# A written issue order, a reciprocal root on VectorE and weights centred by matmuls, in a fused convolution and MLP kernel

## The chip, the cores and the metric

One core of a Trainium2 chip. The metric is the device time of one execution in microseconds (us); a kernel's figure is the median of its runs. All runs quoted here of one kernel lie within 0.15% of each other.

Names used below: PE is TensorE, PEld its weight loads, DVE VectorE, ACT ScalarE, POOL GpSimd, SP the sync engine that issues most transfers. "Span" is the profiled execution from first to last record; the run's time is some 2 us longer.

## The reference

```python
def _attn_ref(x, weight):                # x (8, 4224, 192), weight (8 heads, 7 taps)
    w = softmax(weight, axis=-1)         # shortened here
    x_pad = concatenate([zeros((B, 6, D)), x], axis=1)
    # ... a causal convolution of 7 taps along the sequence, one set of taps per 24 columns

def _moe_ref(x, g_ln, w_ch1, w_ch2):     # w_ch1 (192, 768), w_ch2 (768, 192), g_ln (192)
    mu = np.mean(x, axis=-1, keepdims=True)
    var = np.mean((x - mu) ** 2, axis=-1, keepdims=True)
    xn = (x - mu) / np.sqrt(var + 1e-06) * g_ln
    ch = np.maximum(xn @ w_ch1, 0.0) @ w_ch2
    return (x + ch).astype(np.float32)
```

The MLP weights arrive as 64-bit floats and are turned into 32-bit floats on the core. The mean need not be subtracted from x: both kernels put g and the subtraction into w1 ("centring": each column of g*w1 minus its mean), and multiply by 1/sqrt(var) after the down projection, since the ReLU commutes with a positive factor.

## The kernel before

The sequence is split into groups of 11 rows per partition, 24 groups. For each group DVE does the convolution (56 instructions), a 32x32 block transpose and the statistics; PE does `up` (w1 in four row quadrants of 32), ACT the ReLU, PE `down`, DVE the eviction with the factor and the residual.

```python
    def to_float32(dst, raw, n):            # 10 DVE instructions over n columns
        ...
    def prepare_w1():
        to_float32(w1f, raw1, NW1)          # NW1 = 1152
        ...                                 # share = g / D, a [128, 128] constant
        for r in range(2):
            ...
            nc.tensor.matmul(mean[r][:, 0:FH], share[:, 0, :], w1f[:, fs], start=True, stop=False)
            nc.tensor.matmul(
                mean[r][:, 0:FH], share[rows, 1, :], w1f[rows, F:NW1], start=False, stop=True
            )
        ...                                 # DVE: w1f = g * w1f - mean
        nc.sync.dma_start(out=w1c[0:P, :], in_=w1f[:, 0:F])       # w1c lies in DRAM
        ...
        for q in range(NQ):                 # and back, a copy for each quadrant
            (nc.sync, nc.scalar)[q % 2].dma_start(
                out=w1[C * q : C * q + C, :, :], in_=w1c.rearrange("(c d) f -> d c f", d=C)
            )

    def stats(g):
        ...
        nc.scalar.activation(r, v, AF.Sqrt, bias=eps)
        nc.vector.reciprocal(r, r)
        ...                                 # one Newton step on DVE

    def up(g):
        for f in range(NF):
            ph = [psum.tile([P, 512], F32, tag="ps", name=f"ph{g}_{f}_{q}") for q in range(NQ)]
            for c in range(NC):
                for q in range(NQ):
                    rows = slice(C * q, C * q + C)
                    nc.tensor.matmul(ph[q][:, 0:W], w1[rows, c, fs], t[rows, :, c, :], ...)
            ...                             # four ReLUs on ACT

    prepare_w1()
    conv(0); transpose(0); stats(0)
    to_float32(w2flat, raw2, NW2)
    for g in range(NG):                     # the framework's scheduler orders each engine
        load_x(g + 2); up(g)
        conv(g + 1); transpose(g + 1); stats(g + 1)
        down(g)
```

## Time and profile before

| | before |
|---|---|
| time, median of the first 3 runs | 1126.13 us |
| span of the profiled run | 1123.8 us |
| PE stream of 24 groups | 1036.9 us |
| first `up` matmul | 52.2 us |
| PE held in `up` of group 0 | 24.2 us |
| PE end to span end | 5.2 us |

PE is the bound from about 103 us on; all that a change can win without touching the matmuls of the groups is in the first 103 us and the last 5. The lines that carry this are in the prediction. A line of the timeline is read so: start, duration, engine, source line, operation, output<-inputs, form, count; then in brackets how long the engine was idle before it and who released it.

### The profile page before, as it was taken

To read this page: it belongs to the slowest core of one execution; us is meant where nothing else is said; L and a number is where in the kernel's file an instruction comes from. 1 tells how busy PE (TensorE), PEld (TensorE's weight loads), DVE (VectorE), ACT (ScalarE), POOL (GpSimd) and SP (SyncE) were. 2 spreads that over 40 slices of the span, in tenths; PEclk is the share of its full clock that TensorE was granted. 3 is DMA by queue.
4 is the path that set the end of the run, shared out by engine and by line. 5 is a ranking of instruction groups with operands and counts; after the bars stand their busy time and mean duration, and the time that the engine had idled before them with its cause. 6 is when DMAs were issued, how large, how long until landed. Compare 5 with 4: busy or idle time off the path is not lost.

```text
span 1123.8 us, 23187 instructions
## 1 busy us (share of the span) xinstructions
PE 1048.6 (93%) x10088; PEld 872.8 (78%) x10088; DVE 795.2 (71%) x2145; ACT 230.4 (21%) x603; POOL 9.1 (1%) x12
## 2 busy tenths in 40 slices
PE   1246999999999999999999999999999999999998
PEld 0126897887887887987987978978978878879877
DVE  5999778678587687696695796785886876875001
ACT  0012213113123123022122132131131131230220
POOL 0000000000000000000000000000000000000000
PEclk9987999999999999999999999999999999999999
DMA  7601211210211210211210211112102110000010
GB/s 263 165 1 61 100 60 54 85 61 41 99 60 41 99 60 40 99 61 41 99 61 40 85 62 54 60 54 86 60 40 99 61 40 40 1 40 40 1 40 39
DMA packets 10950, 72.85 MB, mean 65 GB/s; under 512 B 1640, under 2 KB 2536, under 8 KB 4704
## 3 DMA queue, kind: packets, MB, share of 16 engines
q1 hardware_dynamic: 8880, 67.63, 16.3%
q10 hardware_dynamic: 1968, 3.74, 1.2%
q8 instruction: 79, 1.29, 0.5%
q14 instruction: 23, 0.19, 0.1%
HBM read 44.82 MB, written 26.54 MB: 63 GB/s over the span
## 4 chain that ended last, share of the span: by engine, by line
PE 92%; DVE 6%; DMA 1%; ACTq 0%; ACT 0%; issue 0%; DVEq 0%
PE po L315 46%; PE ph L297 45%; DVE y L244 3%; DMA raw<-in_moe_w_ch_dram 1%; DVE st L261 1%; DVE yt L251 0%; DVE y L239 0%; PE mean L203 0%; PE mean L204 0%; DVE mant L154 0%; DVE scale L146 0%; DVE power L135 0%; DVE power L142 0%; DVE mant L150 0%; DVE rest L159 0%; DVE mant L158 0%
## 5 line engine op out<-in xcount | busy, mean ns | idle before, releaser
L297 PE MATMUL ph<-yt,w 32*128 32x352 f32 x6912 | 523.2, 458 | 46.4 <-ACT ht L302 24.2
L315 PEld LDWEIGHTS po<-w,ht 128*128 128x128 f32 x3168 | 513.5, 190 | 13.5 <-issue 11.8
L315 PE MATMUL po<-w,ht 128*128 128x192 f32 x3168 | 522.3, 327 | 0.0
L297 PEld LDWEIGHTS ph<-yt,w 32*128 32x128 f32 x6912 | 357.3, 186 | 205.1 <-ACT ht L302 24.8
L244 DVE SCALAR_TENSOR_TENSOR y<-xg,taps,y 128x264 f32<-128x264 f32 x1152 | 467.7, 485 | 0.0
L302 ACT ACTIVATE ht<-ph 128x352 f32<-128x352 f32 x576 | 220.4, 469 | 330.0 <-PE ph L297 330.0
L320 DVE SCALAR_TENSOR_TENSOR y<-po,r,y 128x192 f32<-128x192 f32 x264 | 95.0, 408 | 233.6 <-PE po L315 233.6
L272 ACT ACTIVATE r<-v,eps 128x11 f32<-128x11 f32 x24 | 7.3, 303 | 504.5 <-DVE y L320 454.5
L239 DVE TENSOR_SCALAR y<-xg,taps 128x264 f32<-128x264 f32 x192 | 54.8, 355 | 61.9 <-DMA out_dram<-y 61.9
L261 DVE BATCH_NORM_STATS2 st<-y 128x6 f32<-128x192 f32 x264 | 70.9, 344 | 0.8
L251 DVE STREAM_TRANSPOSE yt<-y 128x2112 f32<-128x2112 f32 x24 | 56.9, 2370 | 0.0
L203 PE MATMUL mean<-w1f,share 128*128 128x384 f32 x4 | 3.3, 928 | 23.6 <-DVE w1f L164 23.6
L203 PEld LDWEIGHTS mean<-w1f,share 128*128 128x128 f32 x4 | 1.0, 310 | 24.7 <-DVE w1f L164 23.6
L84 POOL MEMSET xg<- 1x1152 f32 x8 | 8.9, 1111 | 792.6 <-DVE y L244 792.3
L273 DVE RECIPROCAL r<-r 128x11 f32<-128x11 f32 x24 | 5.4, 225 | 8.1 <-ACT r L272 8.1
L135 DVE TENSOR_SCALAR power<-raw 128x1152 uint32<-128x1152 uint32 x2 | 1.5, 756 | 7.4 <-DMA raw<-in_moe_w_ch_dram 7.4
L277 DVE SCALAR_TENSOR_TENSOR d<-v,eps,d 128x11 f32<-128x11 f32 x24 | 5.5, 230 | 0.8
L272 ACT ACT_TABLE_LOAD x1 | 1.3, 1283 | 19.9 <-DVE y L244 19.9
L264 DVE TENSOR_TENSOR d<-st 128x11 f32<-128x11 f32 x24 | 4.2, 177 | 0.7
L280 DVE TENSOR_SCALAR d<-d 128x11 f32<-128x11 f32 x24 | 4.1, 172 | 0.8
L283 DVE TENSOR_TENSOR r<-r,d 128x11 f32<-128x11 f32 x24 | 4.1, 170 | 0.8
L276 DVE TENSOR_TENSOR d<-r 128x11 f32<-128x11 f32 x24 | 4.1, 169 | 0.8
(33 smaller groups left out, 40.9 us busy)
## 6 DMA issues: line engine op xcount, KB each, us to landing
xg<-in_x_dram SPq DMA_DIRECT2D x16, 1632.0 KB, 6.6
out_dram<-y SPq DMA_DIRECT2D x24, 1056.0 KB, 4.0
xg<-in_x_dram SPq DMA_DIRECT2D x8, 1056.0 KB, 5.3
xg<-in_x_dram SPq DMA_DIRECT2D x8, 504.0 KB, 6.2
raw<-in_moe_w_ch_dram ACTq DMA_DIRECT2D x1, 1152.0 KB, 12.5
w<-w1c SPq DMA_DIRECT2D x2, 576.0 KB, 10.0
w<-w1c ACTq DMA_DIRECT2D x2, 576.0 KB, 10.4
raw<-in_moe_w_ch_dram ACTq DMA_DIRECT2D x1, 768.0 KB, 7.5
```

Source lines behind the costliest of these rows:

```text
L84: nc.gpsimd.memset(t[0:1, 0:PAD, :], 0.0)
L239: nc.vector.tensor_scalar(out=y[g][:, :, cs], in0=t[:, 0:J, cs], scalar1=tap, scalar2=None, op0=ALU.mult,)
L244: nc.vector.scalar_tensor_tensor(out=y[g][:, :, cs], in0=t[:, k : k + J, cs], scalar=tap, in1=y[g][:, :, cs], op0=ALU.mult, op1=ALU.add,)
L251: nc.vector.transpose(yt[g].rearrange("p j c t -> p (j c t)"), y[g].rearrange("p j d -> p (j d)"))
L261: nc.vector.bn_stats(out=st[:, j, :], in_=y[g][:, j, :])
L272: nc.scalar.activation(r, v, AF.Sqrt, bias=eps)
L273: nc.vector.reciprocal(r, r)
L277: nc.vector.scalar_tensor_tensor(out=d, in0=v, scalar=eps, in1=d, op0=ALU.add, op1=ALU.mult)
L297: nc.tensor.matmul(ph[q][:, 0:W], w1[rows, c, fs], t[rows, :, c, :], start=(c == 0), stop=(c == NC - 1),)
L302: nc.scalar.activation(ht[g][:, f, :, q, :], ph[q][:, 0:W].rearrange("p (j t) -> p j t", t=C), AF.Relu)
L315: nc.tensor.matmul(dst, t[:, f, j, :, :].rearrange("p q t -> p (q t)"), w2[:, f, :], start=(f == 0), stop=(f == NF - 1),)
L320: nc.vector.scalar_tensor_tensor(out=y[g][:, j, :], in0=dst, scalar=rstd[g][:, j : j + 1], in1=y[g][:, j, :], op0=ALU.mult, op1=ALU.add,)
```

## The change

Its intent: start PE earlier, close the hole after group 0, shorten the end. Cut to its core:

```diff
+    sizes = [7, 8, rest // 2, rest - rest // 2]        # batch 0: 7, 8, 9, 9 rows
+    ctx.enter_context(tc.manual_schedule())            # the order of the source is kept
     ...                                                # w1 loaded in parts, x(0) before w2
-        ... 10 DVE instructions per conversion
+        ... 6 DVE and 2 ACT instructions (split_words, join_words)
-        mean matmuls, DVE corrections, to DRAM and back
+    m = setup.tile([P, NC, NQ, C], F32, name=f"centre{i}")   # mask: identity - 1/D, four times
+    nc.gpsimd.memset(m, -1.0 / D); nc.gpsimd.affine_select(m[p0:p1], ...)
+    nc.scalar.mul(flat, flat, gk)
+    def centre_w1():
+        for f in range(NF):
+            r, o = divmod(f * P, FH)
+            rows = slice(Q * r, Q * r + Q)
+            for c0, c1 in ((0, 4), (4, NC)):
+                pw = psum.tile([P, 512], F32, tag="ps", name=f"pw{f}_{c0}")
+                for c in range(c0, c1):
+                    dst = pw[:, (c - c0) * P : (c - c0 + 1) * P]
+                    nc.tensor.matmul(
+                        dst, centre[0][:, c, :], w1f[:, 1 + r, o : o + P], start=True, stop=False
+                    )
+                    nc.tensor.matmul(
+                        dst, centre[1][rows, c, :], w1f[rows, 0, o : o + P],
+                        start=False, stop=True,
+                    )
+                nc.scalar.copy(w1[:, c0:c1, f * P : f * P + P], ...)
     ...
-        nc.scalar.activation(r, v, AF.Sqrt, bias=eps)
-        nc.vector.reciprocal(r, r)
+        ... shift, subtract from 0x5F3759DF, three Newton steps, all on DVE
     ...
+        ends = (n,) if g + 1 < NG else (4, 8, 10, n)    # the last store in four pieces
     ...
-    prepare_w1(); conv(0); transpose(0); stats(0); to_float32(w2flat, raw2, NW2)
+    conv(0); centre_w1(); transpose(0)
+    parts = split_words(raw2, "2"); join_words(w2flat, raw2, *parts)
     for g in range(NG):
         ...
+        if g == 0: conv(1)
         up(g)
         if g + 1 < NG:
-            conv(g + 1); transpose(g + 1); stats(g + 1)
+            if g > 0: conv(g + 1)
+            transpose(g + 1)
+        stats(g)
         down(g)
```

w1 has 192 rows, 128 + 64, so each of its 36 outputs is the sum of a matmul over 128 rows and one over 64 rows.

More of the change, by code (lines that the diff above doesn't have):

```diff
@@ L9 @@
 U32 = mybir.dt.uint32
+I32 = mybir.dt.int32
 AF = mybir.ActivationFunctionType
@@ L53 @@
     NQ = P // C
-    W = J * C
-    assert D == P + Q and S % P == 0 and R % J == 0 and W <= 512 and NF % 2 == 0
-    groups = [(b, j0) for b in range(B) for j0 in range(0, R, J)]
+    FH = F // 2
+    assert D == P + Q and S % P == 0 and J * C <= 512 and NF % 2 == 0
+    groups = []
+    for b in range(B):
+        sizes = [J] * (R // J) + [R % J] * (R % J > 0)
+        if b == 0:
+            rest = R - 15
+            sizes = [7, 8, rest // 2, rest - rest // 2]
+        j0 = 0
+        for n in sizes:
+            groups.append((b, j0, n))
+            j0 += n
+        assert j0 == R and max(sizes) <= J
     NG = len(groups)
+    ctx.enter_context(tc.manual_schedule())
     xr = x.rearrange("b (p r) d -> b p (r d)", p=P)
@@ L64 @@
     setup = ctx.enter_context(tc.tile_pool(name="setup", bufs=1))
-    dram = ctx.enter_context(tc.tile_pool(name="dram", bufs=1, space=bass.MemoryType.DRAM))
     xpool = ctx.enter_context(tc.tile_pool(name="xin", bufs=3))
@@ L76, in load_x @@
     def load_x(g):
-        b, j0 = groups[g]
+        b, j0, n = groups[g]
         t = xpool.tile([P, J + PAD, D], F32, tag="xg", name=f"xg{g}")
@@ L81, in load_x @@
         if j0:
-            nc.sync.dma_start(out=flat, in_=xr[b, :, (j0 - PAD) * D : (j0 + J) * D])
+            nc.sync.dma_start(
+                out=flat[:, 0 : (n + PAD) * D], in_=xr[b, :, (j0 - PAD) * D : (j0 + n) * D]
+            )
             return
         nc.gpsimd.memset(t[0:1, 0:PAD, :], 0.0)
-        nc.sync.dma_start(out=flat[:, PAD * D :], in_=xr[b, :, 0 : J * D])
-        for p0, p1 in ((1, 16), (16, P)):
+        nc.sync.dma_start(out=flat[:, PAD * D : (PAD + n) * D], in_=xr[b, :, 0 : n * D])
+        for p0, p1 in ((16, P), (1, 16)):
             nc.sync.dma_start(
@@ L92, with load_w1 @@
     taps = consts.tile([P, H, K], F32, name="taps")
+    ga = consts.tile([P, 1], F32, name="ga")
+    gb = consts.tile([P, 1], F32, name="gb")
+    raw1 = setup.tile([P, 3, FH, 2], U32, name="raw1")
+    raw2 = setup.tile([P, NF * D, 2], U32, name="raw2")
+    w1_words = moe_w_ch1.bitcast(U32)
+    w2_words = moe_w_ch2.bitcast(U32)
+    g_col = moe_g_ln.rearrange("(d o) -> d o", o=1)
+    def load_w1(r):
+        nc.scalar.dma_start(
+            out=raw1[:, 1 + r, :, :].rearrange("p f w -> p (f w)"),
+            in_=w1_words[0:P, 2 * FH * r : 2 * FH * (r + 1)],
+        )
     nc.sync.dma_start(
@@ L95 @@
     )
-    FH = F // 2
-    NW1 = F + FH
-    NW2 = NF * D
-    raw1 = setup.tile([P, NW1, 2], U32, name="raw1")
-    raw2 = setup.tile([P, NW2, 2], U32, name="raw2")
-    ga = consts.tile([P, 1], F32, name="ga")
-    gb = consts.tile([P, 1], F32, name="gb")
-    w1_words = moe_w_ch1.bitcast(U32)
-    w2_words = moe_w_ch2.bitcast(U32)
-    g_col = moe_g_ln.rearrange("(d o) -> d o", o=1)
-    nc.scalar.dma_start(
-        out=raw1[:, 0:F, :].rearrange("p f w -> p (f w)"), in_=w1_words[0:P, :]
-    )
+    load_w1(0)
     for r in range(2):
         nc.scalar.dma_start(
-            out=raw1[Q * r : Q * r + Q, F:NW1, :].rearrange("p f w -> p (f w)"),
+            out=raw1[Q * r : Q * r + Q, 0, :, :].rearrange("p f w -> p (f w)"),
             in_=w1_words[P:D, 2 * FH * r : 2 * FH * (r + 1)],
         )
-    nc.scalar.dma_start(out=ga, in_=g_col[0:P, :])
+    load_w1(1)
+    load_x(0)
+    nc.gpsimd.dma_start(out=ga, in_=g_col[0:P, :])
     for r in range(2):
-        nc.scalar.dma_start(out=gb[Q * r : Q * r + Q, :], in_=g_col[P:D, :])
-    load_x(0)
-    load_x(1)
-    nc.scalar.dma_start(
+        nc.gpsimd.dma_start(out=gb[Q * r : Q * r + Q, :], in_=g_col[P:D, :])
+    nc.sync.dma_start(
         out=raw2.rearrange("p (c d) w -> p c (d w)", d=D),
@@ L125, with split_words @@
     )
-    def to_float32(dst, raw, n):
-        lo, hi = raw[:, :, 0], raw[:, :, 1]
-        power = setup.tile([P, n], U32, tag="power", name="power")
-        scale = setup.tile([P, n], U32, tag="scale", name="scale")
-        mant = setup.tile([P, n], U32, tag="mant", name="mant")
-        rest = setup.tile([P, n], U32, tag="rest", name="rest")
+    load_x(1)
+    low = consts.tile([P, 1], F32, name="low")
+    nc.vector.memset(low, -896.0 * (1 << 23))
+    def split_words(raw, name):
+        n = raw.shape[1]
+        hi = raw[:, :, 1]
+        mant = setup.tile([P, n], I32, name="mant" + name)
+        power = setup.tile([P, n], I32, name="power" + name)
+        high = setup.tile([P, n], F32, name="high" + name)
+        scale = setup.tile([P, n], I32, name="scale" + name)
+        nc.vector.tensor_single_scalar(mant.bitcast(U32), hi, 0xFFFFF, op=ALU.bitwise_and)
+        nc.scalar.activation(high, mant, AF.Relu, scale=2.0**-20, bias=1.0)
         nc.vector.tensor_scalar(
-            out=power, in0=hi, scalar1=20, scalar2=0x7FF,
+            out=power.bitcast(U32), in0=hi, scalar1=20, scalar2=0x7FF,
             op0=ALU.logical_shift_right, op1=ALU.bitwise_and,
@@ L139, in to_float32, with join_words @@
         nc.vector.tensor_scalar(
-            out=power, in0=power, scalar1=896.0, scalar2=0.0, op0=ALU.subtract, op1=ALU.max
+            out=power, in0=power, scalar1=896.0, scalar2=1151.0, op0=ALU.max, op1=ALU.min
         )
-        nc.vector.tensor_scalar(
-            out=power, in0=power, scalar1=255.0, scalar2=float(1 << 23),
-            op0=ALU.min, op1=ALU.mult,
+        nc.scalar.activation(scale, power, AF.Relu, scale=float(1 << 23), bias=low)
+        return high, scale
+    def join_words(dst, raw, high, scale):
+        lo, hi = raw[:, :, 0], raw[:, :, 1]
+        nc.vector.scalar_tensor_tensor(
+            out=high, in0=lo, scalar=2.0**-52, in1=high, op0=ALU.mult, op1=ALU.add
         )
         nc.vector.scalar_tensor_tensor(
-            out=scale, in0=hi, scalar=0x80000000, in1=power,
+            out=scale.bitcast(U32), in0=hi, scalar=0x80000000, in1=scale.bitcast(U32),
             op0=ALU.bitwise_and, op1=ALU.bitwise_or,
         )
-        nc.vector.tensor_scalar(
-            out=mant, in0=hi, scalar1=0xFFFFF, scalar2=3,
-            op0=ALU.bitwise_and, op1=ALU.logical_shift_left,
-        )
-        nc.vector.scalar_tensor_tensor(
-            out=mant, in0=lo, scalar=29, in1=mant,
-            op0=ALU.logical_shift_right, op1=ALU.bitwise_or,
-        )
-        nc.vector.tensor_single_scalar(mant, mant, 0x3F800000, op=ALU.bitwise_or)
-        nc.vector.tensor_single_scalar(rest, lo, 0x1FFFFFFF, op=ALU.bitwise_and)
-        nc.vector.scalar_tensor_tensor(
-            out=dst, in0=rest, scalar=2.0**-52, in1=mant.bitcast(F32),
-            op0=ALU.mult, op1=ALU.add,
-        )
-        nc.vector.tensor_tensor(dst, dst, scale.bitcast(F32), op=ALU.mult)
-    eps = consts.tile([P, 1], F32, name="eps")
-    nc.vector.memset(eps, 1e-6)
+        nc.vector.tensor_tensor(dst, high, scale.bitcast(F32), op=ALU.mult)
+    w1f = setup.tile([P, 3, FH], F32, name="w1f")
+    raw1a = raw1[:, 0:2].rearrange("p s f w -> p (s f) w")
+    raw1b = raw1[:, 2]
     wmax = consts.tile([P, H], F32, name="wmax")
@@ L176 @@
     nc.scalar.activation(taps, taps, AF.Exp)
+    parts_a = split_words(raw1a, "1a")
     nc.vector.tensor_reduce(wsum, taps, axis=AX.X, op=ALU.add)
@@ L182 @@
     )
-    w1f = setup.tile([P, NW1], F32, name="w1f")
+    join_words(w1f[:, 0:2].rearrange("p s f -> p (s f)"), raw1a, *parts_a)
+    parts_b = split_words(raw1b, "1b")
+    join_words(w1f[:, 2], raw1b, *parts_b)
     w1 = consts.tile([P, NC, F], F32, name="w1")
-    w2flat = consts.tile([P, NW2], F32, name="w2")
+    w2flat = consts.tile([P, NF * D], F32, name="w2")
     w2 = w2flat.rearrange("p (c d) -> p c d", d=D)
-    w1c = dram.tile([D, F], F32, name="w1c")
-    def prepare_w1():
-        to_float32(w1f, raw1, NW1)
-        share = setup.tile([P, 2, P], F32, name="share")
-        for i, g in enumerate((ga, gb)):
-            nc.vector.tensor_scalar(
-                out=share[:, i, :], in0=g.to_broadcast([P, P]),
-                scalar1=1.0 / D, scalar2=None, op0=ALU.mult,
-            )
-        mean = [psum.tile([P, 512], F32, tag="ps", name=f"mean{r}") for r in range(2)]
-        for r in range(2):
-            fs = slice(FH * r, FH * r + FH)
-            rows = slice(Q * r, Q * r + Q)
-            nc.tensor.matmul(mean[r][:, 0:FH], share[:, 0, :], w1f[:, fs], start=True, stop=False)
-            nc.tensor.matmul(
-                mean[r][:, 0:FH], share[rows, 1, :], w1f[rows, F:NW1], start=False, stop=True
-            )
-        for r in range(2):
-            fs = slice(FH * r, FH * r + FH)
-            rows = slice(Q * r, Q * r + Q)
-            nc.vector.scalar_tensor_tensor(
-                out=w1f[:, fs], in0=w1f[:, fs], scalar=ga, in1=mean[r][:, 0:FH],
-                op0=ALU.mult, op1=ALU.subtract,
-            )
-            nc.vector.scalar_tensor_tensor(
-                out=w1f[rows, F:NW1], in0=w1f[rows, F:NW1], scalar=gb[rows, :],
-                in1=mean[r][rows, 0:FH], op0=ALU.mult, op1=ALU.subtract,
-            )
-        nc.sync.dma_start(out=w1c[0:P, :], in_=w1f[:, 0:F])
-        for r in range(2):
-            nc.scalar.dma_start(
-                out=w1c[P:D, FH * r : FH * r + FH], in_=w1f[Q * r : Q * r + Q, F:NW1]
-            )
-        for q in range(NQ):
-            (nc.sync, nc.scalar)[q % 2].dma_start(
-                out=w1[C * q : C * q + C, :, :], in_=w1c.rearrange("(c d) f -> d c f", d=C)
-            )
@@ new lines @@
+    centre = []
+    for i, (gk, spans) in enumerate(((ga, ((0, P, 0),)), (gb, ((0, Q, P), (Q, P, P))))):
+        m = setup.tile([P, NC, NQ, C], F32, name=f"centre{i}")
+        nc.gpsimd.memset(m, -1.0 / D)
+        for p0, p1, base in spans:
+            nc.gpsimd.affine_select(
+                out=m[p0:p1], in_=m[p0:p1], pattern=[[-C, NC], [0, NQ], [-1, C]],
+                compare_op=ALU.not_equal, fill=1.0 - 1.0 / D, base=base, channel_multiplier=1,
+            )
+        flat = m.rearrange("p c q i -> p (c q i)")
+        nc.scalar.mul(flat, flat, gk)
+        centre.append(flat.rearrange("p (c o) -> p c o", c=NC))
@@ new lines, in centre_w1 @@
+    def centre_w1():
+        for f in range(NF):
+            r, o = divmod(f * P, FH)
+            rows = slice(Q * r, Q * r + Q)
+            for c0, c1 in ((0, 4), (4, NC)):
[4 more added lines that the diff above has]
+                        dst, centre[0][:, c, :], w1f[:, 1 + r, o : o + P], start=True, stop=False
+                    )
+                    nc.tensor.matmul(
+                        dst, centre[1][rows, c, :], w1f[rows, 0, o : o + P],
+                        start=False, stop=True,
+                    )
+                nc.scalar.copy(
+                    w1[:, c0:c1, f * P : f * P + P],
+                    pw[:, 0 : (c1 - c0) * P].rearrange("p (c f) -> p c f", f=P),
+                )
@@ L229 @@
     y, yt, rstd = {}, {}, {}
     def conv(g):
+        n = groups[g][2]
         t = xg.pop(g)
@@ L237, in conv @@
                 tap = taps[:, h, k : k + 1]
-                if k == 0:
+                if k == 0 and g < 2:
+                    nc.scalar.mul(y[g][:, 0:n, cs], t[:, 0:n, cs], tap)
+                elif k == 0:
                     nc.vector.tensor_scalar(
-                        out=y[g][:, :, cs], in0=t[:, 0:J, cs], scalar1=tap, scalar2=None,
+                        out=y[g][:, 0:n, cs], in0=t[:, 0:n, cs], scalar1=tap, scalar2=None,
                         op0=ALU.mult,
@@ L244, in conv @@
                     nc.vector.scalar_tensor_tensor(
-                        out=y[g][:, :, cs], in0=t[:, k : k + J, cs], scalar=tap,
-                        in1=y[g][:, :, cs], op0=ALU.mult, op1=ALU.add,
+                        out=y[g][:, 0:n, cs], in0=t[:, k : k + n, cs], scalar=tap,
+                        in1=y[g][:, 0:n, cs], op0=ALU.mult, op1=ALU.add,
                     )
     def transpose(g):
+        n = groups[g][2]
         yt[g] = tpool.tile([P, J, NC, C], F32, tag="yt", name=f"yt{g}")
         nc.vector.transpose(
-            yt[g].rearrange("p j c t -> p (j c t)"), y[g].rearrange("p j d -> p (j d)")
+            yt[g][:, 0:n].rearrange("p j c t -> p (j c t)"),
+            y[g][:, 0:n].rearrange("p j d -> p (j d)"),
         )
     def stats(g):
+        n = groups[g][2]
         st = spool.tile([P, J, nc.vector.BN_STATS_DIM], F32, tag="st", name=f"st{g}")
-        d = spool.tile([P, J], F32, tag="d", name=f"d{g}")
-        v = spool.tile([P, J], F32, tag="v", name=f"v{g}")
-        r = spool.tile([P, J], F32, tag="r", name=f"r{g}")
-        for j in range(J):
+        dt = spool.tile([P, J], F32, tag="d", name=f"d{g}")
+        vt = spool.tile([P, J], F32, tag="v", name=f"v{g}")
+        rt = spool.tile([P, J], F32, tag="r", name=f"r{g}")
+        d, v, r = dt[:, 0:n], vt[:, 0:n], rt[:, 0:n]
+        for j in range(n):
             nc.vector.bn_stats(out=st[:, j, :], in_=y[g][:, j, :])
-        nc.vector.tensor_tensor(d, st[:, :, 1], st[:, :, 4], op=ALU.subtract)
-        nc.vector.tensor_tensor(v, st[:, :, 2], st[:, :, 5], op=ALU.add)
+        nc.vector.tensor_tensor(d, st[:, 0:n, 1], st[:, 0:n, 4], op=ALU.subtract)
+        nc.vector.tensor_tensor(v, st[:, 0:n, 2], st[:, 0:n, 5], op=ALU.add)
         nc.vector.scalar_tensor_tensor(
@@ L271, in stats @@
         )
-        nc.scalar.activation(r, v, AF.Sqrt, bias=eps)
-        nc.vector.reciprocal(r, r)
-        nc.vector.tensor_tensor(d, r, r, op=ALU.mult)
-        nc.vector.scalar_tensor_tensor(
-            out=d, in0=v, scalar=eps, in1=d, op0=ALU.add, op1=ALU.mult
+        nc.vector.tensor_scalar(v, v, scalar1=1e-6, scalar2=None, op0=ALU.add)
+        nc.vector.tensor_single_scalar(
+            d.bitcast(U32), v.bitcast(U32), 1, op=ALU.logical_shift_right
         )
         nc.vector.tensor_scalar(
-            out=d, in0=d, scalar1=-0.5, scalar2=1.5, op0=ALU.mult, op1=ALU.add
-        )
-        nc.vector.tensor_tensor(r, r, d, op=ALU.mult)
-        rstd[g] = r
+            out=r.bitcast(I32), in0=d.bitcast(I32), scalar1=-1.0, scalar2=float(0x5F3759DF),
+            op0=ALU.mult, op1=ALU.add,
+        )
+        for _ in range(3):
+            nc.vector.tensor_tensor(d, r, r, op=ALU.mult)
+            nc.vector.scalar_tensor_tensor(
+                out=d, in0=d, scalar=-0.5, in1=v, op0=ALU.mult, op1=ALU.mult
+            )
+            nc.vector.scalar_tensor_tensor(
+                out=r, in0=d, scalar=1.5, in1=r, op0=ALU.add, op1=ALU.mult
+            )
+        rstd[g] = rt
     ht = {}
     def up(g):
+        n = groups[g][2]
         t = yt.pop(g)
@@ L297, in up @@
                     nc.tensor.matmul(
-                        ph[q][:, 0:W], w1[rows, c, fs], t[rows, :, c, :],
+                        ph[q][:, 0 : n * C], w1[rows, c, fs], t[rows, 0:n, c, :],
                         start=(c == 0), stop=(c == NC - 1),
@@ L302, in up @@
                 nc.scalar.activation(
-                    ht[g][:, f, :, q, :], ph[q][:, 0:W].rearrange("p (j t) -> p j t", t=C), AF.Relu
+                    ht[g][:, f, 0:n, q, :],
+                    ph[q][:, 0 : n * C].rearrange("p (j t) -> p j t", t=C), AF.Relu,
                 )
     def down(g):
-        b, j0 = groups[g]
+        b, j0, n = groups[g]
         t = ht.pop(g)
-        for i0 in range(0, J, 2):
-            js = range(i0, min(i0 + 2, J))
+        yg = y.pop(g)
+        ends = (n,) if g + 1 < NG else (4, 8, 10, n)
+        done = 0
+        for i0 in range(0, n, 2):
+            js = range(i0, min(i0 + 2, n))
             po = psum.tile([P, 512], F32, tag="ps", name=f"po{g}_{i0}")
@@ L320, in down @@
                 nc.vector.scalar_tensor_tensor(
-                    out=y[g][:, j, :], in0=dst, scalar=rstd[g][:, j : j + 1],
-                    in1=y[g][:, j, :], op0=ALU.mult, op1=ALU.add,
-                )
-        nc.sync.dma_start(
-            out=outr[b, :, j0 * D : (j0 + J) * D], in_=y.pop(g).rearrange("p j d -> p (j d)")
-        )
-    prepare_w1()
+                    out=yg[:, j, :], in0=dst, scalar=rstd[g][:, j : j + 1],
+                    in1=yg[:, j, :], op0=ALU.mult, op1=ALU.add,
+                )
+            if js[-1] + 1 in ends:
+                end = js[-1] + 1
+                nc.sync.dma_start(
+                    out=outr[b, :, (j0 + done) * D : (j0 + end) * D],
+                    in_=yg[:, done:end].rearrange("p j d -> p (j d)"),
+                )
+                done = end
     conv(0)
+    centre_w1()
     transpose(0)
-    stats(0)
-    to_float32(w2flat, raw2, NW2)
+    parts = split_words(raw2, "2")
+    join_words(w2flat, raw2, *parts)
     for g in range(NG):
@@ L336 @@
             load_x(g + 2)
+        if g == 0:
+            conv(1)
         up(g)
         if g + 1 < NG:
-            conv(g + 1)
+            if g > 0:
+                conv(g + 1)
             transpose(g + 1)
-            stats(g + 1)
+        stats(g)
         down(g)
```

## The prediction

> **What bounds the kernel now.** I read the page first (busy shares and the slices), then the chain that ended last, then the stretches of the first 100 us, then the timeline of those. From the page, the slices of 28 us each:
>
> ```profile
> PE 1048.6 (93%) x10088; PEld 872.8 (78%) x10088; DVE 795.2 (71%) x2145; ACT 230.4 (21%) x603; POOL 9.1 (1%) x12
> PE   1246999999999999999999999999999999999998
> DVE  5999778678587687696695796785886876875001
> ```
>
> PE is the bound from the fifth slice to the end; only the first 4 slices and the last have holes. The chain of work that ended last, in order of time, says how regular the rest is:
>
> ```profile
> 31.34 17.87 DVE y L244 x44
> ...
> 66.42 19.39 DVE y L244 x48
> ...
> 93.08 10.13 PE ph L297 x94
> 103.21 21.65 PE po L315 x132
> 124.86 21.51 PE ph L297 x288
> 146.37 21.69 PE po L315 x132
> ```
>
> From 103 us on it is PE alone, 21.51 + 21.69 = 43.20 us for each of 24 groups: 24 x 43.20 = 1036.9 us of pure matmul stream. The span is 1123.8, so 86.9 us are not that stream. Where they are (timeline of the start, PE and its releasers; columns: start, us, engine, line, operation):
>
> ```profile
> 52.22 16.65 PE L297 MATMUL ph<-yt,w 32*128 32x352 f32 x192 [22.22 <-DVE yt L251]
> 92.38 0.30 ACT L272 ACTIVATE r<-v,eps 128x11 f32<-128x11 f32 x1 [29.04 <-DVE v L269]
> 92.58 2.92 ACT L302 ACTIVATE ht<-ph 128x352 f32<-128x352 f32 x8
> 93.08 10.13 PE L297 MATMUL ph<-yt,w 32*128 32x352 f32 x96 [24.20 <-ACT ht L302]
> ```
>
> Four pieces: (a) 52.2 us until the first up matmul: weight conversion on DVE, then the 11-row convolution, then the transpose at 49.8. (b) 24.2 us in which PE waits for the ReLU (ht): ACT waits 29.0 us for the Sqrt of group 1, which stands ahead of the ReLUs of group 0 in its order and needs the whole convolution of group 1 on DVE (L269). (c) Slow clock: the first 192 matmuls took 16.65 us where 192 x 21.51/288 = 14.34 would do (2.3 lost), the 96 after the hole 10.13 for 7.17 (3.0 lost); the stretches give a granted clock of 0.69, 0.50 and 0.62 from 70 to 100 us. (d) The end: PE stops at 1118.6, the span ends 5.2 later. Sum 52.2 + 24.2 + 5.3 + 5.2 = 86.9, so it closes.
>
> [...] four 32-row weight loads come every 0.585 us from 52.97 to 56.49 and every 0.299 (21.51/72) later.[...] the Sqrt holds ACT 29.0 us.[...] po loads (mean 190 ns, busy 162 per load) hide under 164 ns matmuls.[...] Here a 96 KB store to DRAM landed after 2.4 us and the last 1056 KB store after 4.0 (median)[...].
>
> **The change part by part.**
>
> *PE stream.* Groups of batch 0 become 7, 8, 9, 9 rows in place of 11, 11, 11. Up costs 36 sets per group; a set at 352 columns is 21.51/36 = 597 ns[...]. At 224, 256, 288, 288 columns: 384, 438, 491, 491 ns, so 13.8 + 15.8 + 17.7 + 17.7 = 65.0; 21 more groups x 21.51 = 451.7. Down is 264 rows x 6 x 328.6 ns = 520.6. Sum 1037.3: one more group costs nothing worth naming.
>
> *Before the first up matmul.* Order and split of the weight loads: only 768 KB of w1 are needed first. Before, the 768 KB load landed 7.5 us after its issue at 0.74, all of w1 only at 13; I take 9.5 us. The conversion drops from 10 DVE operations over 1152 columns to 6 and two on ACT, in parts of 768 and 384 columns. DVE start-to-start, from the timeline: a one-source operation over 1152 takes 0.67, over 264 0.283, so about 0.168 + 0.436 n/1000; a two-source one 1.27 and 0.406, so 0.149 + 0.973 n/1000. Part a: 3 x 0.50 + 3 x 0.90; part b: 3 x 0.34 + 3 x 0.52; taps 0.8; some 1 us of waits on ACT. Sum 8.6: w1f is ready at some 18 (before 23.6). conv(0) then has 48 two-source operations over 168 columns, 0.313 each, 15.0 us (before 19.5); its 8 first taps go to ACT (about 0.3 each). DVE: 18 + 15.0 = 33, transpose 1.5: yt(0) at 34.8 in place of 52.2.
>
> *The centring by matmuls* replaces mean matmuls, DVE corrections and a DRAM round trip (10 us landing, hidden under conv before). It adds 36 x 2 matmuls of 128 columns, so 144 PE instructions ahead of up(0). [...] mean matmuls in the cold state had 0.147 us per instruction over their streaming of 640, which is 0.07 warm. So 0.125 to 0.18, I take 0.15: 21.6 us, plus 2 for the cold start: 23.5. From 17.5 that ends at **41**. This, not yt(0) at 34.8, sets the start of up(0): centring on the critical path is the term that I am least sure of (16 to 32 us). PE is then warm, so the 2.3 of (c) are not paid again.
>
> *The hole (b).* The reciprocal root leaves ACT: no Sqrt, no second table load, nothing of DVE ahead of the ReLUs. w2's ACT part (2 x 1.05) and 8 first taps of conv(1) (2.4) stand ahead of the ReLUs of group 0; two sets of 4 PSUM banks buy 4.7 us of PE work, so about 2 us remain as a stall. All of 24.2 + 3.0 goes but these 2.
>
> *Is DVE then in time?* w2 joins at 41 + 2.3 + 3.9 = 47, conv(1) (48 x 0.336 = 16.1) and transpose end at 65; PE needs yt(1) at 41 + 2 + 13.8 + 13.8 = 71. conv(2) begins after the last eviction of group 0 at 72, ends with its transpose at 93, with PE there at 102. Slack 6 to 9 us. Steady state: the root costs 16 small operations at 0.17 to 0.26 against 9 and an ACT step; DVE per 11-row group 21.7 + 2.3 + 3.0 + 3.7 + 4.0 = 34.7 under 43.2. Not the bound.
>
> *Last store in pieces.* The last piece is one row, 96 KB, landing in some 2.4 instead of 4.0: saves 1.7 of (d).
>
> *Sum*: 41 + 2 + 1037.3 + 5.2 - 1.7 = 1083.8 of span. Medians are 2.3 above the span (1126.1 against 1123.8), the profiled run 1.8: **1085.5**, I say 1085, 3.8% faster.
>
> **Rivals.** (1) The centring is much dearer: loads not hidden under 128-column matmuls[...]. At 0.25 per instruction it is 36 us + 2, and up(0) starts at 56: 1100. For it: the 0.147 gap of the mean matmuls. Against it: po hides loads under 164 ns. (2) A new wait at the start: GpSimd builds the centring masks (two fills, three selects, of which this trace has no price; a fill of 1152 columns took 1.1 us) and g comes by GpSimd's queue; if these end at 22 instead of 16, ACT, and behind it the first taps and DVE, shift by 6: 1091. (3) DVE becomes the bound in the short first groups, because fixed order puts w2's join behind the ACT copies of the centring: slack 6, so a loss of up to some 5 only if conversions run 10 us late. (4) Fixed order breaks the steady state, with ReLU or evictions behind other work: 25 x 1 us would be 25 us and eat half the gain. Against: 8.5 us of DVE slack, ACT at 21%. (5) The start is not worth it at all because loads set it: the first 10 us moved 206 GB/s, the next 326; all the data before was in at 13.7, so no.
>
> **Range and chances.** The centring's 16 to 32 us gives 1078 to 1094; early ends by faster loads perhaps 4 below, masks or PSUM waits 4 to 6 above: 1074 to 1099. Even with rival 1 it stays over 2% faster (1104 is the line). Both (1) and (2), or (4), would be needed to miss: 6%. Slower than before would need a new 40 us: 1%.
>
> **What would show it.** First up matmul near 41, preceded by 144 matmul instructions from about 17.5; no idle PE over 3 us after it; no ACT wait for DVE statistics; up of the first group 13.8 us and groups of 43.2 later; PE's end to span's end near 3.5. Wrong if centring takes over 32 us, if PE waits for yt(1) or yt(2), or if a group in the middle takes over 43.5.

The sum is 41 + 2 + 1037.3 + 5.2 - 1.7 = 1083.8 us of span and 1085 of time, but two of its terms stand as estimates. The times of the short groups (384, 438 and 491 ns, 65.0 us of the 1037.3) follow nearly as well from the trace: 21.51 us scaled by columns, over 36 sets, is 380, 435 and 489, and the changed kernel took 437.5 and 490.8 for the last two (15.75 and 17.67 us for 36 sets). The 0.15 us per instruction of the centring (21.6 us of the 41) is left with the mean matmuls alone: 0.147 us over a streaming of 0.640, which is 384 columns at the 1.67 ns that the trace before shows at the slow clock (see below). That 0.07 of it would be left warm is an estimate, half of 0.147.

## The result, and the profile after

The changed kernel took 1118.87 us (median of 4), the kernel before 1125.96 in the same rounds: ratio 0.9937, 95% interval 0.992 to 0.9954: a gain of 0.6%, clear of noise, where 3.8% was predicted. The range of 1074 to 1099 was missed by 20 us.

The page of the changed kernel, its first lines and slices of 28 us:

```profile
PE 1092.0 (98%) x10512; PEld 917.0 (82%) x10512; DVE 822.5 (74%) x2362; ACT 242.0 (22%) x638; POOL 14.7 (1%) x20
PE   2999999999999999999999999999999999999998
PEclk9999999999999999999999999999999999999999
```

PE is busy for 98% of the span instead of 93%: the holes are closed as intended. But the busy time grew by 43 us (1048.6 to 1092.0). A busy engine is not a productive one, and the chain of work that ended last, in order of time, says with what:

```profile
by line: PE po L348 46.6%; PE ph L325 46.5%; PE pw L230 2.3%; PE pw L233 2.3%; DMA raw<-in_moe_w_ch_dram 1.1%; DVE w1f L180 0.1%; ACT centre L219 0.1%; issue 0.1%; DVE scale1a L176 0.1%; DVE high1a L173 0.1%; DVE mant1a L159 0.1%; DVE power
...
74.27 16.20 PE ph L325 x288
90.47 13.85 PE po L348 x84
104.32 15.75 PE ph L325 x288
120.07 15.80 PE po L348 x96
...
249.91 21.51 PE ph L325 x288
```

The first `up` starts at 74.3 us, 22 later than before and 33 later than predicted. The centring (pw, lines 230 and 233) holds the chain with 4.6% of it. The groups after it are as predicted: 13.85 and 15.75 for the short ones, 21.51 for the full. Only the first `up` is off, 16.20 instead of 13.8, and that is a clue. The timeline where the centring starts follows. Its first line is DVE's first use of w1, its second PE's first matmul of the centring, released by the first mask (centre):

```profile
14.38 0.56 DVE L159 TENSOR_SCALAR mant1a<-raw 128x768 uint32<-128x768 uint32 x1 [7.25 <-DMA raw<-in_moe_w_ch_dram]
...
22.01 0.80 PE L230 MATMUL pw<-w1f,centre 128*128 128x128 f32 x2 [22.01 <-ACT centre L219]
...
23.56 0.79 PE L230 MATMUL pw<-w1f,centre 128*128 128x128 f32 x2
24.29 0.79 PE L233 MATMUL pw<-w1f,centre 64*128 64x128 f32 x2
25.01 0.79 PE L230 MATMUL pw<-w1f,centre 128*128 128x128 f32 x2
...
70.58 0.79 PE L233 MATMUL pw<-w1f,centre 64*128 64x128 f32 x2
```

A program matmul of 32-bit floats is two PE instructions (x2). One starts every 0.723 us (65 of them from 23.56 to 70.58), early as late: 0.361 per instruction, where 0.15 was predicted, and no change in 52 us. The time by stretch, predicted and measured:

| | predicted | measured |
|---|---|---|
| w1's first 768 KB on the core | 9.5 us | 14.3 |
| centring starts | 17.5 | 22.0 |
| centring takes | 23.5 | 52.2 |
| first `up` matmul | 41 | 74.2 |
| lost to a slow start of `up` | 0 | 2.4 |
| stall for the first ReLUs | 2 | 0 |
| rest of PE's stream | 1037.3 | 1037.4 |
| PE end to span end | 3.5 | 3.3 |
| span | 1083.8 | 1117.3 |

So of the 33.5 us missed, 28.7 are the rate of the centring and 4.5 the start of it. Two clues say what the rate is made of. First, the kernel before had mean matmuls of the same kind over 384 columns, at 0.787 us per instruction. The difference to 0.361 is 0.426 us for 256 columns, 1.66 ns a column. That is the slow clock: the trace of the kernel before has a clock record of 0.5 from 73.73 to 97.63 us, under which `up` takes 0.587 us for 352 columns (1.67 ns a column), and 0.297 (0.84) under the record of 1.0 that follows. Second, 0.148 us per instruction are left over in both, whatever the columns. And the first `up` starts at half rate (0.373 us for 224 columns, 1.67 ns a column) and goes over to 0.189 (0.85) some 5 us later, so at the end of the centring the clock was still slow. The granted clock on the page says 1.00 all the while (22.0 to 74.2 us, and 74.2 to 79.0); it doesn't show this state, as the trace has no clock record there. The records that it has agree with the rates: the first of the changed kernel, of 1.0, begins only at 79.06 us, 4.9 us after `up` started. Where the record of 1.0 begins is given below as "clock record".

### The profile page after: what moved, and what is told of

It is laid out like the page before. It is cut to its first block, busy times and chain, and to the rows that moved or that the text cites. A ratio compares the mean times of both kernels' runs of the same rounds, so it can differ in the third digit from the quotient of the medians.

```text
span 1117.3 us, 24334 instructions
## 1 busy us (share of the span) xinstructions
PE 1092.0 (98%) x10512; PEld 917.0 (82%) x10512; DVE 822.5 (74%) x2362; ACT 242.0 (22%) x638; POOL 14.7 (1%) x20
## 4 chain that ended last, share of the span: by engine, by line
PE 98%; DMA 1%; DVE 1%; ACTq 0%; ACT 0%; issue 0%; DVEq 0%
PE po L348 47%; PE ph L325 46%; PE pw L230 2%; PE pw L233 2%; DMA raw<-in_moe_w_ch_dram 1%; DVE w1f L180 0%; ACT centre L219 0%; DVE scale1a L176 0%; DVE high1a L173 0%; DVE power1a L165 0%; DVE mant1a L159 0%; ACTq L132 0%; DVE power1a L161 0%; DVE y L353 0%; ACTq L122 0%
## 5 line engine op out<-in xcount | busy, mean ns | idle before, releaser
L325 PE MATMUL ph<-yt,w 32*128 32x352 f32 (+3 forms) x7200 | 520.8, 445 | 0.0
L261 DVE SCALAR_TENSOR_TENSOR y<-xg,taps,y 128x264 f32<-128x264 f32 (+3 forms) x1200 | 473.8, 477 | 0.9 <-ACT y L254 0.9
L330 ACT ACTIVATE ht<-ph 128x352 f32<-128x352 f32 (+3 forms) x600 | 222.7, 457 | 791.6 <-PE ph L325 791.6
L269 DVE STREAM_TRANSPOSE yt<-y 128x2112 f32<-128x2112 f32 (+3 forms) x25 | 57.3, 2290 | 0.9
L256 DVE TENSOR_SCALAR y<-xg,taps 128x264 f32<-128x264 f32 (+1 forms) x184 | 51.4, 351 | 0.0
L230 PE MATMUL pw<-w1f,centre 128*128 128x128 f32 x72 | 28.6, 501 | 22.0 <-ACT centre L219 22.0
L230 PEld LDWEIGHTS pw<-w1f,centre 128*128 128x128 f32 x72 | 18.0, 310 | 29.9 <-ACT centre L219 22.0
L233 PE MATMUL pw<-w1f,centre 64*128 64x128 f32 x72 | 28.5, 498 | 0.0
L233 PEld LDWEIGHTS pw<-w1f,centre 64*128 64x128 f32 x72 | 18.0, 310 | 8.2 <-issue 7.9
L304 DVE TENSOR_TENSOR d<-r 128x11 f32<-128x11 f32 (+3 forms) x75 | 12.8, 170 | 2.6
```

The costliest lines, as they stand in the source:

```text
L230: nc.tensor.matmul(dst, centre[0][:, c, :], w1f[:, 1 + r, o : o + P], start=True, stop=False)
L233: nc.tensor.matmul(dst, centre[1][rows, c, :], w1f[rows, 0, o : o + P], start=False, stop=True,)
L256: nc.vector.tensor_scalar(out=y[g][:, 0:n, cs], in0=t[:, 0:n, cs], scalar1=tap, scalar2=None, op0=ALU.mult,)
L261: nc.vector.scalar_tensor_tensor(out=y[g][:, 0:n, cs], in0=t[:, k : k + n, cs], scalar=tap, in1=y[g][:, 0:n, cs], op0=ALU.mult, op1=ALU.add,)
L269: nc.vector.transpose(yt[g][:, 0:n].rearrange("p j c t -> p (j c t)"), y[g][:, 0:n].rearrange("p j d -> p (j d)"),)
L304: nc.vector.tensor_tensor(d, r, r, op=ALU.mult)
```

## The experiments

The theory: each pass (one PE instruction) leaves its weight load exposed (not hidden behind the matmul before it), and an array that streams only 59% of the time (0.213 of 0.361, 128 columns at 1.67 ns) never gets its clock opened (raised from 0.5 to 1.0). Why the load is exposed was open: the change between 128 and 64 rows, 64 rows in themselves, the short passes, or the slow clock itself.

### e1_cols384: the centring over 384 columns at a time

```diff
-        for f in range(NF): ... for c0, c1 ...: for c ...:      # 72 matmuls of 128 columns
+        for r in range(2):
+            for c in range(NC):                                  # 24 matmuls of 384 columns
+                nc.tensor.matmul(pw[:, 0:FH], centre[0][:, c, :], w1f[:, 1 + r, :], ...)
+                nc.tensor.matmul(pw[:, 0:FH], centre[1][rows, c, :], w1f[rows, 0, :], ...)
```

> The changed kernel with the same centring done over 384 columns at once: 24 matmuls (48 PE instructions) in place of 72 (144). In the changed kernel one PE instruction of 128 columns takes 0.361 us; before, one of 384 columns took 0.787. [...] both look like the slow clock, with 0.148 us per instruction on top that does not grow with columns. Theory A (a fixed cost per pass, the weight load not hidden, and the slow clock kept all the way): 48 x 0.787 = 37.8 us in place of 52.2, first up matmul near 60, time 1104 to 1105. Theory B (the clock opens once streaming fills 81% of the time instead of 59%): the first 4 to 5 us slow, the rest near 0.39 per instruction, 21 us in all, first up near 43, time near 1088. Theory C (the number of columns is all that counts, no fixed cost): no change, 1119.

Measured: 1104.12 us, ratio 0.9805 to the kernel before. Theory A, to the microsecond. The timeline of PE:

```profile
31.13 1.65 PE L227 MATMUL pw<-w1f,centre 128*128 128x384 f32 x2
32.71 1.65 PE L230 MATMUL pw<-w1f,centre 64*128 64x384 f32 x2
...
57.93 1.65 PE L230 MATMUL pw<-w1f,centre 64*128 64x384 f32 x2
59.51 15.92 PE L318 MATMUL ph<-yt,w 32*128 32x224 f32 x288
```

1.577 us per program matmul from the first to the last: 1.28 of streaming at the slow clock (2 x 384 columns at 1.67 ns) and 0.297 exposed, as in the 128-column case (0.723 - 0.427 = 0.296). Short passes are not the cause of the exposure. Streaming now fills 81% of the time, and 38 us of it didn't open the clock either (clock record: 63.66 us, 4.2 us into `up`).

### e2_rows128: the second matmul over 128 rows as well

```diff
-                        dst, centre[1][rows, c, :], w1f[rows, 0, o : o + P],
+                        dst, centre[1 + r][:, c, :], w1f[:, 0, o : o + P],   # zeros in the other 64 rows
```

> The changed kernel with the second matmul of each centring pair over all 128 rows, its mask zero in the half that does not belong to it, so that 128-row and 64-row passes no longer alternate. Theory A2 (the weight load is exposed because the two passes of a pair use different sets of rows): the load hides behind the matmul as it does in the down projection, 0.21 to 0.25 us per instruction or less, centring 18 to 36 us, time 1086 to 1103. Theory A (exposed whatever the rows, because of the slow clock or the short passes): 0.361 as before, centring 52, time 1119 to 1120 (one more mask to multiply, 0.9 us).

Measured: 1085.50 us, ratio 0.9639. The arithmetic is the same, with zeros added, and 33.4 us are gone. The timeline of PE:

```profile
24.64 0.63 PE L234 MATMUL pw<-w1f,centre 128*128 128x128 f32 x2
25.07 0.60 PE L231 MATMUL pw<-w1f,centre 128*128 128x128 f32 x2
25.50 0.40 PE L234 MATMUL pw<-w1f,centre 128*128 128x128 f32 x2
25.73 0.39 PE L231 MATMUL pw<-w1f,centre 128*128 128x128 f32 x2
25.96 0.39 PE L234 MATMUL pw<-w1f,centre 128*128 128x128 f32 x2
...
40.51 4.82 PE L326 MATMUL ph<-yt,w 32*128 32x224 f32 x96 [0.32 <-DVE yt L270]
```

At first a matmul starts every 0.43 us, which is pure streaming at the slow clock (2 x 128 columns at 1.67 ns, 0.427): no load is seen any more. From 25.5 us, some 3.6 us after the start, one starts every 0.223: the clock has opened (clock record: 25.51). `up` starts at 40.5, where the prediction had 41.

### e5_grouped384: 64-row matmuls kept, but not alternated

Of e2_rows128 one could still say that 64-row loads are exposed in themselves. This run keeps them and changes the order of e1_cols384; with it six sums stay open in six banks, and ACT's copies come after them.

```diff
             for c in range(NC):
                 nc.tensor.matmul(pw[c][:, 0:FH], centre[0][:, c, :], w1f[:, 1 + r, :], ...)
+            for c in range(NC):
                 nc.tensor.matmul(pw[c][:, 0:FH], centre[1][rows, c, :], w1f[rows, 0, :], ...)
```

> As e1_cols384, with the passes grouped: for each half, the six 128-row matmuls first, then the six 64-row ones, each accumulating in its own bank. The same 48 instructions, loads and rows, but 4 changes of the row set in place of 48 program matmuls that each followed one of the other kind. Theory S (the change of rows exposes the load): passes follow at streaming pace, 0.64 us each while slow, the clock opens after about 4 us as in e2_rows128, 18 us in all, first up matmul near 40 to 42 (with yt(0) ready at about 40), time 1084 to 1087. Theory R (a 64-row load is exposed in itself, whatever comes before it): half or all of the 0.3 us per pair remains and the clock stays slow, 35 to 38 us, time 1101 to 1105.

Measured: 1084.44 us, ratio 0.963. The timeline of PE:

```profile
21.73 5.61 PE L227 MATMUL pw<-w1f,centre 128*128 128x384 f32 x12 [21.73 <-ACT centre L219]
27.27 4.13 PE L231 MATMUL pw<-w1f,centre 64*128 64x384 f32 x12
31.33 4.14 PE L227 MATMUL pw<-w1f,centre 128*128 128x384 f32 x12
35.40 4.13 PE L231 MATMUL pw<-w1f,centre 64*128 64x384 f32 x12
```

Twelve instructions over 64 rows take 4.06 us from start to start (27.27 to 31.33), 0.339 each, and the same over 128 rows. In the trace's single records a matmul starts every 0.322 us, but the two at the change of 27.27 come 0.416 and 0.427 us after the one before: 0.20 us are lost at the change, none between changes. At the change the weight load starts only with its own matmul (27.266 and 27.268 us); elsewhere it starts a whole matmul ahead (26.531 for the matmul at 26.852). The same instructions in the alternating order took 37.8 us, in this order 17.7. So 64 rows are not dear in themselves; the change between 128 rows and 64 is. A change of rows as such is not: `up` goes through four sets of 32 rows without a pause, four loads every 0.299 us. e2_rows128, which had both matmuls of a pair one after the other into the same bank, also rules out that accumulating straight onto the last result was what held it.

### e3_warm: the clock opened beforehand

```diff
+    warm_up(34)            # 34 x four 32-row matmuls of 352 columns on a constant, unused
     conv(0)
     centre_w1()
```

> The changed kernel with PE kept streaming on constants (34 sets of four 32-row matmuls, 352 columns, results unused) from about 2 us until the centring can start. Theory G ([...] the centring keeps the array too little busy): the first instructions of the centring take about 0.18 us each, then[...] they fall back to 0.361 and stay there; time 1114 to 1118. Theory N (the array was never woken, but once awake the centring keeps it so): 0.18 all the way, 26 us, time near 1093. Theory L (0.361 has nothing to do with the clock[...]): 0.361 from the first, time 1119.

Measured: 1097.90 us, ratio 0.9749, near theory N's 1093 (0.208 per instruction instead of its 0.18); G and L are out. The timeline of PE:

```profile
1.33 21.91 PE L250 MATMUL pd<-warm 32*128 32x352 f32 x272 [1.33 <-DVE warm L152]
23.18 0.49 PE L232 MATMUL pw<-w1f,centre 128*128 128x128 f32 x2
23.60 0.49 PE L235 MATMUL pw<-w1f,centre 64*128 64x128 f32 x2
24.01 0.49 PE L232 MATMUL pw<-w1f,centre 128*128 128x128 f32 x2
...
52.76 0.48 PE L235 MATMUL pw<-w1f,centre 64*128 64x128 f32 x2
```

The alternating centring, unchanged, now takes 0.4165 us per matmul to its end, 30 us in all. That is below the 0.427 which streaming alone would need at the slow clock, so the clock was open (one clock record, unbroken from 4.45 to 1096.71 us), and it stayed open for 30 us although streaming filled only about half of the time (0.223 of 0.4165, with the pace of e2_rows128 as the streaming). The exposed part is 0.193 (0.4165 less the 0.223 of e2_rows128) instead of 0.296. So it took more to open the clock than to keep it open: 81% of streaming at the slow clock did not open it (e1_cols384), about half at the open clock kept it. What decides on it, the runs don't show.

With this the 52.2 us can be split: hiding the loads alone would give 72 x 0.427 = 30.8 (an estimate from 0.427, in no run), an open clock alone gives 30.0 (this run), both give 18 (e2_rows128, its slow start included).

### e6_dram_w1: one part undone, w1 centred as before

```diff
-    centre = [] ... def centre_w1(): ...            # masks, 72 matmuls, 12 copies
+    mean matmuls; corrections on DVE inside conv(0), before its fifth tap; w1c to DRAM and back
```

> The changed kernel with one part undone: w1 centred as before (mean matmuls, two corrections on DVE per half, placed inside conv(0), then to DRAM and back in quadrants). The centring leaves PE. If the 52.2 us of centring are what ate the gain: w1f at 22, means by 29, corrections by 33, DRAM out 2.4 and back 10.4 us, first up matmul near 46, time near 1090, some 29 less than the changed kernel. If something else of the start holds PE (DVE, loads), less than half of that: over 1104.

Measured: 1093.16 us, ratio 0.9706; 25.7 less than the changed kernel. The timeline of PE:

```profile
41.85 1.35 PE L332 MATMUL ph<-yt,w 32*128 32x224 f32 x4 [13.38 <-DMA w<-w1c]
47.49 17.17 PE L332 MATMUL ph<-yt,w 32*128 32x224 f32 x284 [4.29 <-DMA w<-w1c]
```

The old round trip through DRAM is better than the new centring as it was written, by 25.7 us; three us of the expected gain went because the last quadrants arrived at 47.5 instead of 46 and the clock was slow again (17.17 for some 13.6, an estimate from the 15.75 of 256 columns). So without the new centring the rest of the change takes 32.9 us off the kernel before (1126.05 in the same rounds).

### e4_root_only and e7_act_root: what closed the hole

The prediction said that the root on DVE closes the 24.2 us hole. One run does that part alone on the kernel before, the other undoes it alone in the changed kernel.

```diff
 # e4_root_only, in the kernel before
-        nc.scalar.activation(r, v, AF.Sqrt, bias=eps)
-        nc.vector.reciprocal(r, r)
-        ... one Newton step
+        ... shift, subtract, three Newton steps
 # e7_act_root, in the changed kernel: the other way round
```

> The kernel before with only the reciprocal root moved from ACT to DVE (shift, subtract, three Newton steps), all else as it was, the scheduler's order included. If the hole of 24.2 us was ACT held by the Sqrt, it closes, and with it the 3.0 us of slow clock after it: 1126 - 27 = 1099, PE starting at 52 as before. The same would say that the rest of the change costs some 20 us. Rival (the ReLUs of group 0 were going to wait for DVE work anyway, or the scheduler puts something else ahead of them): little change, 1120 to 1126.

> The changed kernel with the root back on ACT (Sqrt, then reciprocal and one Newton step on DVE), the written order kept: statistics of group g after the ReLUs of group g. Theory O (the order closes the hole, the root does not matter, as e4_root_only suggests from the other side): 1118 to 1121. Rival (the root on DVE was needed): PE waits again for ReLUs behind the Sqrt, in the first groups or in each, over 1125.

Measured: e4_root_only 1124.95 us (ratio 0.9989, interval 0.9974 to 1.0004), e7_act_root 1118.75 (0.9934). Neither moved. The expectation for the first, 1099, was a miss. Its wait, then the timeline of PE, then of DVE:

```profile
PE ph L302 <- DVE y L325: 23.3, 1, 23.3
```

```profile
75.50 21.78 PE L320 MATMUL po<-w,ht 128*128 128x192 f32 x132
...
97.21 0.86 PE L302 MATMUL ph<-yt,w 32*128 32x352 f32 x4
...
121.39 24.89 PE L302 MATMUL ph<-yt,w 32*128 32x352 f32 x284 [23.32 <-DVE y L325]
```

```profile
98.02 16.25 DVE L245 SCALAR_TENSOR_TENSOR y<-xg,taps,y 128x264 f32<-128x264 f32 x40
...
120.60 3.67 DVE L325 SCALAR_TENSOR_TENSOR y<-po,r,y 128x192 f32<-128x192 f32 x11
```

In e4_root_only the ReLUs no longer wait: `up` of group 0 runs through, and `down` ends at 97.2. But DVE, in the order that the scheduler chose, does the convolution of group 2 before it evicts group 0 (from 120.6), so PE now waits 23.3 us for its banks. The hole has moved from one side of `down` to the other. DVE had two convolutions to finish in that stretch in either case. In the changed kernel the order is written: on ACT the root of a group after the ReLUs of the same group, on DVE the evictions of group 0 before the convolution of group 2. With it the Sqrt may as well sit on ACT; this is all that PE waits for in e7_act_root:

```profile
PE pw L232 <- ACT centre L221: 22.0, 1, 22.0
```

So the root on DVE is worth nothing measurable by itself. What closed the hole is the written order together with the smaller first groups (7 and 8 rows in place of 11); no run separates these two.

### e8_best: the fix, and the loads in order of need

```diff
 # on e2_rows128
-    SP: taps, x(0), w2, x(1)     ACT: w1 in four parts     POOL: g
+    ACT: the first 768 KB of w1, then x(0)     SP: taps, g, the rest of w1, w2, x(1)
+    masks multiplied before the last third of w1 is converted
```

> e2_rows128 (all passes over 128 rows) with the first loads put in order of need: w1's first 768 KB alone at the head of ACT's queue, x(0) behind it, g and w1's last third on SP's queue, w2 and x(1) behind; the masks multiplied before the last third is converted. Theory D (w1's first part landed at 14.2 instead of the predicted 9.5 because x(0) shared the engines with it): it lands by 8 us, all that follows starts 4 to 7 us earlier, 1077 to 1081. Rival (landing does not depend on what else is on its way, or x(0) now comes late for the convolution): 1083 to 1086.

Measured: 1077.68 us, ratio 0.9572, correct: 4.3% less than the kernel before, the fastest of all runs. The timeline:

```profile
8.68 0.56 DVE L160 TENSOR_SCALAR mant1a<-raw 128x768 uint32<-128x768 uint32 x1 [3.45 <-DMA xg<-in_x_dram]
...
13.99 0.77 PE L231 MATMUL pw<-w1f,centre 128*128 128x128 f32 x2 [13.99 <-DVE w1f L181]
...
32.98 4.82 PE L326 MATMUL ph<-yt,w 32*128 32x224 f32 x96 [0.83 <-DVE yt L270]
39.28 10.07 PE L326 MATMUL ph<-yt,w 32*128 32x224 f32 x192 [1.48 <-ACT ht L331]
```

The conversion of w1 starts at 8.7 instead of 14.4, with the same data in the start as a whole. So the late landing of the changed kernel was company on the transfer engines (DMA share 1.02 to 1.05 from 8 to 14.3 us), not the transfer itself. (The view names x(0) as releaser; w1's own first pieces landed 6.3 and 6.8 us after their issues at 0.7 to 1.8, by the list of transfers.) Which company it was, x(0) or w1's last third, this run doesn't separate, as it moved both. The first `up` is at 33.0, where it waits 0.83 us for yt(0), that is for DVE's convolution. The second line of `up` shows the stall for the first ReLUs that the prediction put at 2 us: 1.48.

## Why the prediction was wrong, by its own steps

1. **What bounds the kernel**: right. The four pieces of 86.9 us were the right ones, and 1037.3 us of stream was measured as 1037.4.
2. **The centring by matmuls**: the step that failed. "So 0.125 to 0.18, I take 0.15: 21.6 us, plus 2 for the cold start: 23.5." Measured: 0.361 per instruction, 52.2 us; the prediction's own sign of being wrong, over 32 us, came true. The text had the evidence in hand, the 0.147 us over streaming of the mean matmuls, and halved it "warm" without asking why the mean matmuls had not been warm. Two assumptions were false: that loads hide here as they do in `down` (alternating 128 and 64 rows exposes them: e2_rows128, e5_grouped384), and that work without a pause opens the clock after some 4 us (2 us lost at half rate; not at 59% or 81% streaming: the changed kernel and e1_cols384, 52 and 38 us). With both false terms put right, e2_rows128 took 1085.50 us against the 1085 predicted. That closeness is partly luck: its load was 4.7 us late, its centring 5 us faster than assumed.
3. **Rival 1** named the exposed loads, at too small a size, 0.25 per instruction and 1100. With the open clock that size would have been about right (e3_warm: 0.208 and 1097.90); the slow clock was not in it.
4. **The loads**: 9.5 us assumed, 14.3 measured; 4.5 us of the miss. x(0) and w1's last third were on the transfer engines with it; with both moved, DVE began on w1 at 8.68 us instead of 14.38 (e8_best).
5. **The hole (b)**: it went, as predicted, but the reason was wrong: not the root (e4_root_only, e7_act_root), but the written order together with the smaller first groups, which no run separates. The 2 us of stall did not appear in the changed kernel, where `up` ran at half rate until 79.06 us and ACT began the ReLUs at 79.55; with the open clock it is there, 1.5 us in e2_rows128, e5_grouped384 and e8_best.
6. **DVE in time, steady state**: right; full groups take 43.2 us, no wait of PE for yt after the first group, in e2_rows128 and e8_best neither.
7. **Last store in pieces**: right, 3.3 us against 3.5 predicted and 5.2 before; the last piece landed after 1.6 us instead of 2.4.
8. **The slow start of `up`**, "PE is then warm, so the 2.3 of (c) are not paid again": wrong for the same reason as step 2, 2.4 us.

Left open: what opens the clock (81% of streaming in e1_cols384 did not, about 100% in e2_rows128 did), and why a load is not started ahead across a change between 128 and 64 rows; the runs show that it isn't, not by what mechanism.

## What to carry to other kernels

When a sum over K is split unevenly (128 + 64 rows), don't alternate the two kinds of matmul: group them by their number of rows (e5_grouped384: 19.7 us less than e1_cols384), or pad the short one with zeros to the full rows (e2_rows128: 33.4 less than the changed kernel). Check that matmuls put on the critical path at the start of a kernel run at the open clock: divide columns by time rather than trust a busy share, and if there is nothing dense to open it, stream something else first (e3_warm: 21.0 less). When one wait is removed, ask what the same engine would do next in its order; a hole whose real cause is another engine's order only moves.
